# Attention and two MoE layers on one core: row sums in four streams, W_out blocks in the keys' place, and a new order

## Chip, cores and metric

One Trainium2 chip, one core. The metric is device microseconds of the core, the median of three runs. The profiled execution is one more run of the same kernel, and every row shown here is of that execution.

## What is computed

```python
def _attn_ref(q, k, v):                       # 2 batches, 12 heads, 448 tokens, head size 64
    scores = np.matmul(q, k.transpose(0, 1, 3, 2)) / np.sqrt(64)
    scores = np.where(np.triu(ones, k=1), -1e9, scores)
    attn = np.exp(scores - scores.max(-1, keepdims=True))
    return np.matmul(attn / (attn.sum(-1, keepdims=True) + 1e-09), v)

x = attn_out as 896 tokens x 768
h = x @ w_in                                  # 768 x 1024
solu = h * softmax(h)
x = layernorm(solu) * g_ln @ w_out            # 1024 x 768
out = relu(x @ w_in2)**2 @ w_out2             # 768 x 2048, 2048 x 768
```

The weights come as float64, read as pairs of 32-bit words.

## The kernel before

**Attention** goes over 12 pairs of heads, pair `i` holding two heads of 64 rows each (`h` is 0 or 1), so that K and Q of both fill 128 partitions. For each pair the kernel does the following, by the names in its order string. `S0a`, `S0b`, `S0c` (line 250) are cheap score products that only serve to find the row maxima, which VectorE (`mxa`, `mxb`, `mxc`, line 265), a transpose on TensorE (`mT`, line 277), ScalarE (`row`, line 282) and two small transfers (`rowd`, lines 294 and 295) turn into a row that a matmul subtracts. `Sa` and `Sb` (lines 308 and 319) are the full-precision scores, `ea1` and `eb1` (line 343) the exponentials on ScalarE, `ka` and `kb` (line 340) the causal mask on GpSimd. `ad` (lines 364 and 366) adds key blocks on GpSimd, so that the row sums need fewer columns on TensorE. `Ua` and `Ub` (line 352) multiply by V, with 64 output rows for each head, and `Us` (line 374) multiplies by ones, which gives the row sums in the second half of the same PSUM tile `U`.

**What follows a pair's sums** is a chain of small steps. `E` (lines 381 and 382) copies sums and products from PSUM to the SBUF tile `E`, of which there are two, and gives the PSUM tile back. `sums` (line 389) moves the sums of the two heads, each a row of 448 on one partition, into a 112x8 tile, one transfer for each head. `recips` (line 395) takes reciprocals on VectorE. `rcd` (line 401) writes them to DRAM, `spread` (line 408, two transfers) reads them back over 64 partitions for each head into the tile `bc`. `norm` (line 416) multiplies on GpSimd, and `x_hi` and `x_lo` (lines 424 and 428) split the result into two words.

**First MoE layer.** `h<t>.<c>` (line 492) adds the products of token tile `t` with the `c`-th of 6 blocks of `w_in`, six matmuls of 512 columns; it needs `x` of pair `c` (first batch), `6 + c` (second batch), or both for tile 3. A finished tile goes through `mx`, `ex`, `mu`, `sq`, `de`, `va`, `pw`, `fa`, `ln`, a transpose `T` (line 617) and a split `Th`, `Tl` (line 631). `lw` loads a block of `w_out` (768 KB, line 125), `of` (lines 150 to 152) makes float32 of it on VectorE, `oh` (line 564) and `ol` (line 567) split it. `y0` and `y1` (line 639) are its products. The second MoE layer (line 774) follows and is written as loops.

**Order.** Up to the second layer the string `SEQ` fixes the order, and with it the order on each engine and on the one queue (SP) from which all transfers are issued: an engine or queue takes its items in that order, and an item that waits holds up all behind it. `fl` items are matmuls on zeros at the start. PSUM holds four tiles in flight; a new one takes the place that was given back longest ago.

**Memory.** Blocks 0 to 5 of `w_out` have their place in the pool `lnp`, which is opened when the attention's last `x_lo` has been emitted, over tiles that the attention uses to its end.

Of the kernel before, what the change touches and what calls it, by code (L numbers as in the profile page):

```python
# [15 lines left out]
NEG = -3.0e38  # L16
UB_ = 3
NWO = 6
AHEAD = 2
NL2 = 3  # L20
LO_POOL = ()
# [3 lines left out]
ATT = ("recips", "rcd", "spread", "norm", "x_hi", "x_lo", "E", "Ua", "Ub", "sums")  # L25

SEQ = """
fl.0 fl.1 fl.2 load_r.0 fl.3 H.0 fl.4 load_r.1 fl.5 H.1 S0c.0 load_r.2 S0a.0 S0b.0 fl.6 fl.7 lq.0 load_r.3 lq.1 mxc.0
lq.4 mxb.0 S0b.1 load_v.0 S0a.1 fl.8 mxa.0 mxb.1 mxa.1 lq.2 mxr.0 Sa.0 H.2 ea1.0 S0c.1 mxc.1 S0a.2 S0b.2 mT.1 row.1
H.3 Sb.0 mxa.2 mxb.2 rowd.1 ka.0 eb1.0 S0c.2 mxc.2 S0b.3 Sb.1 load_r.4 mT.2 mxb.3 Ua.0 lq.5 eb1.1 kb.0 S0c.3 lq.3 ad.0  # L30
row.2 S0a.3 mxc.3 H.4 mxa.3 rowd.2 Sa.1 Ub.0 mT.3 ea1.1 Us.0 S0b.4 row.3 load_v.1 lq.6 wf.0 Sb.2 E.0 eb1.2 mxb.4 Sa.2
load_r.5 kb.1 ea1.2 rowd.3 S0a.4 ka.1 Sa.3 S0c.4 Sb.3 H.5 load_v.2 mxa.4 mxc.4 sums.0 S0a.5 ad.1 mT.4 load_r.6 lq.8
ea1.3 eb1.3 recips.0 mxa.5 row.4 Ua.1 S0b.5 ka.2 H.6 wh.0 Ub.1 S0c.5 lq.7 kb.2 mxb.5 rcd.0 S0a.6 mxc.5 load_v.3 rowd.4
Us.1 Sa.4 ad.2 load_r.7 kb.3 mxa.6 mT.5 E.1 row.5 S0b.6 ea1.4 Ua.2 Sb.4 H.7 mxb.6 S0c.6 spread.0 ka.3 sums.1 eb1.4
ad.3 mxc.6 S0a.7 Ub.2 mT.6 S0b.7 norm.0 kb.4 ld.3 row.6 ka.4 recips.1 mxa.7 x_hi.0 Us.2 rowd.5 E.2 Ua.3 Ub.3 x_lo.0
rcd.1 load_r.8 mxb.7 S0c.7 Sb.5 eb1.5 Sa.5 ad.4 H.8 mxc.7 rowd.6 mT.7 kb.5 Sb.6 ea1.5 wl.0 sums.2 row.7 Us.3 spread.1
recips.2 S0a.8 eb1.6 load_v.4 norm.1 Sa.6 rcd.2 load_r.9 rowd.7 x_hi.1 kb.6 Ua.4 ea1.6 Ub.4 E.3 ka.5 wf.1 S0b.8
spread.2 x_lo.1 Us.4 ka.6 mxa.8 load_r.10 sums.3 norm.2 H.9 S0c.8 ad.5 Sb.7 mxb.8 S0a.9 E.4 mxc.8 Sa.7 recips.3
load_v.5 eb1.7 mxa.9 S0b.9 x_hi.2 mT.8 Ua.5 ea1.7 S0c.9 ad.6 H.10 lq.9 rcd.3 mxb.9 Ub.5 load_v.6 sums.4 mxc.9 x_lo.2
S0b.10 row.8 Ua.6 mT.9 spread.3 load_r.11 Us.5 ka.7 norm.3 recips.4 row.9 mxb.10 rowd.8 wh.1 S0a.10 Ub.6 E.5 mxa.10  # L40
S0c.10 rcd.4 lq.10 kb.7 x_hi.3 load_g.0 H.11 mxc.10 x_lo.3 Us.6 wl.1 Sb.8 eb1.8 mT.10 Sa.8 ad.7 rowd.9 load_v.7 S0b.11
spread.4 sums.5 row.10 norm.4 lq.11 ea1.8 recips.5 mxb.11 E.6 Sa.9 Ua.7 load_v.8 rowd.10 S0a.11 Ub.7 kb.8 x_hi.4
S0c.11 ka.8 ea1.9 Us.7 rcd.5 mxa.11 Sb.9 mxc.11 mT.11 ld.4 row.11 spread.5 Sa.10 sums.6 eb1.9 x_lo.4 Ua.8 wf.2 rowd.11
ad.8 ka.9 Ub.8 h1.0 ea1.10 recips.6 rcd.6 wf.3 norm.5 Sb.10 E.7 ka.10 sums.7 x_hi.5 spread.6 eb1.10 load_v.9 kb.9
Sa.11 Us.8 x_lo.5 wh.2 wl.2 ld.5 Sb.11 h1.1 ea1.11 h1.2 h0.0 load_v.10 norm.6 E.8 recips.7 ad.9 Ua.9 eb1.11 Ub.9
x_hi.6 load_v.11 h0.2 Ua.10 Us.9 rcd.7 h0.1 sums.8 wf.4 kb.10 wh.3 wl.3 wh.4 h0.3 x_lo.6 spread.7 ka.11 wl.4 recips.8
norm.7 E.9 sums.9 wf.5 h0.4 ad.10 Ub.10 rcd.8 wh.5 x_hi.7 recips.9 h1.3 Ua.11 wl.5 x_lo.7 spread.8 h1.4 Us.10 h0.5
kb.11 mx.0 norm.8 rcd.9 E.10 ad.11 x_hi.8 ex.0 Ub.11 sums.10 spread.9 x_lo.8 recips.10 rcd.10 norm.9 de.0 h1.5 h2.0
h2.4 Us.11 mu.0 sq.0 h2.2 spread.10 h2.1 va.0 mx.1 E.11 x_hi.9 sums.11 pw.0 h2.3 fa.0 h2.5 x_lo.9 ln.0 T.0 ex.1
recips.11 norm.10 h3.0 h3.1 h3.3 x_hi.10 Th.0 rcd.11 de.1 spread.11 mx.2 mu.1 h3.2 ex.2 x_lo.10 sq.1 h4.0 Tl.0 norm.11  # L50
x_hi.11 h3.4 mu.2 x_lo.11 va.1 sq.2 de.2 h3.5 va.2 lw.0 pw.1 lw.1 fa.1 h4.1 pw.2 of.0 mx.3 fa.2 h4.4 ex.3 h4.2 ln.1
oh.0 of.1 mu.3 ln.2 ol.0 h4.3 sq.3 h5.0 oh.1 h5.4 de.3 T.1 lw.2 of.2 ol.1 oh.2 va.3 h4.5 pw.3 Th.1 mx.4 ex.4 T.2 h5.3
h5.2 fa.3 ln.3 h5.1 Tl.1 lw.3 Th.2 mu.4 h6.0 of.3 h5.5 lw.4 sq.4 h6.2 mx.5 h6.1 ex.5 oh.3 Tl.2 T.3 mu.5 Th.3 ol.2 h6.4
lw.5 Tl.3 of.4 de.4 de.5 sq.5 va.5 h6.3 pw.5 ol.3 h6.5 mx.6 va.4 fa.5 ex.6 lw.6 y0.0 of.5 pw.4 y0.1 oh.4 y0.2 l2.1
l2.0 oh.5 de.6 ol.4 mu.6 fa.4 of.6 y0.3 ln.4 ol.5 sq.6 oh.6 va.6 y0.4 ol.6 T.4 lw.7 pw.6 Th.4 Tl.4 y0.5 ln.5 fa.6 T.5
y0.6 ln.6 Th.5 of.7 Tl.5 oh.7 T.6 ol.7 Th.6 y0.7 Tl.6 f2.0 y1.0 f2.1 yo.1 y1.1 g2.1 yo.0 g2.0 yp.0 y1.2 yp.1 o2.1 yp.2
yo.2 o2.0 l2.2
"""


def attention_moe_kernel(tc, kq, v, w_in, w_out, g_ln, w_in2, w_out2, out):
# [16 lines left out]
    JP = 112  # L78
# [13 lines left out]
    with es:  # L92
# [21 lines left out]
        moe0, moe1 = ExitStack(), ExitStack()  # L114
# [55 lines left out]
        def give(t):  # L170
            slots.append(slot_of.pop(id(t))[0])
# [5 lines left out]
        with att:  # L177
# [4 lines left out]
            per = att_.enter_context(pool("per", side="right"))  # L182
            lat = att_.enter_context(pool("lat", side="right"))
# [13 lines left out]
            JK = [qk.tile([JP, JP * t + JP], mybir.dt.bfloat16, name=f"JK{t}") for t in range(4)]  # L197

            VR = [per.tile([P, 4, 2, D], F32, name=f"VR{i}") for i in range(3)]
            ONES = per.tile([P, D], F32, name="ONES")  # L200
            PP = [per.tile([P, 2, 512], F32, name=f"PP{i}") for i in range(NPP)]
            SE = per.tile([P, 1], F32, name="SE")
            Q2 = S - P
# [23 lines left out]
            nc.gpsimd.tensor_scalar_mul(NID, ident[0:JP, 0:JP], -1.0)  # L227
            nc.vector.memset(ONES, 1.0)

            mx = {}  # L230
            mr = {}
            UB = {}
            sb = {}
            ee = {}
            rr = {}
# [132 lines left out]
            def row_sum(i):  # L368

                p, pa = ps.pop(i), PP[(2 * i) % NPP]  # L370
                for o, x in ((0, pa[:, :, D : D + P]), (P, p)):
                    n = x.shape[2]
                    for h in range(2):
                        nc.tensor.matmul(
                            UB[i][D * h : D * h + D, 1, o : o + n], ONES, x[:, h], start=o == 0, stop=o > 0
                        )

            def u_out(i):
                U = UB.pop(i)
                ee[i] = lat.tile([P, 2, S], F32, tag="E", name="E", bufs=2)  # L380
                nc.scalar.activation(ee[i][0 : D + 1, 1], U[0 : D + 1, 1, 0:S], AF.Identity, bias=SE[0 : D + 1])
                nc.scalar.copy(ee[i][:, 0], U[:, 0, 0:S])  # L382
                give(U)

            def sums(i):
                c = lat.tile([JP, 8], F32, tag="sc", name="sc", bufs=2)
                for h in range(2):
                    r = ee[i][D * h : D * h + 1, 1].rearrange("o (p j) -> o p j", j=8)
                    nc.sync.dma_start(c[JP // 2 * h : JP // 2 * h + JP // 2], r)
                rr[i] = c  # L390

            def recips(i):
# [20 lines left out]
            def normalise(i):  # L413
                e, bc = ee.pop(i), rr.pop(i)
                x = lat.tile([P, S], F32, tag="x", name="x", bufs=1)
                nc.gpsimd.tensor_tensor(x, e[:, 0], bc, ALU.mult)  # L416
                xs[i] = x

            def x_parts(i):
# [133 lines left out]
            YB1 = {}  # L553

            def load_wo(fi):
                pl, tag, W, o = (M["lnp"], f"wo{fi}", 2 * DM, 0) if fi < NWO else (wst, f"w{fi - NWO}", 2 * DFF, 8)
                WO[fi] = load_w(pl, tag, w_out[fi * P : fi * P + P, :], W, o=o)

            def wo_f(fi):
# [235 lines left out]
            for n in range(NF2, N2):  # L795
                half, fi = blocks2[n]
# [4 lines left out]
                for e, d in sorted(order, key=lambda x: x[1]) if last else order:  # L801
# [3 lines left out]
                    c = ND * half + d  # L805
# [44 lines left out]
```

## Time and profile before

| | us |
|---|---|
| median of 3 runs | 452.52 (452.44 to 453.08) |
| profiled execution | 452.57 |
| its span in the trace | 450.7 |
| TensorE busy | 440.6 (98%) |
| VectorE, ScalarE, GpSimd busy | 265.2, 163.8, 151.5 |

The span is the time from the first to the last instruction that the trace shows; the execution's own time is 1.87 us longer. Busy time of TensorE counts a matmul to its modelled end, and matmuls overlap, so that a short wait can vanish behind the end of the matmul before.

### The profile page before, as it was taken

The numbers are of one execution on the slowest core, as the hardware profiler recorded it, in microseconds if no ns is written. First come the engines' busy times: TensorE is split into PE (matmuls) and PEld (weight loads), VectorE is DVE, ScalarE is ACT, GpSimd is POOL, SyncE is SP. The second block draws the span as 40 slices with busy tenths as digits, with TensorE's granted clock in tenths as the row PEclk, the third lists the DMA queues.
The fourth block names the chain that finished last, engine by engine and source line by source line (L and its number), as shares of the span: only waits on it lengthen the run. The fifth ranks groups of instructions, "written<-read, shape, count | busy, mean of one in ns | idle before, by whom it ended". The sixth has DMA issues, their size and how long they took to land.

```text
span 450.7 us, 6365 instructions
## 1 busy us (share of the span) xinstructions
PE 440.6 (98%) x2439; PEld 372.7 (83%) x2439; DVE 265.2 (59%) x511; ACT 163.8 (36%) x223; POOL 151.5 (34%) x145
## 2 busy tenths in 40 slices
PE   8999899999998999999999999999999999999996
PEld 6666455666886899888999999999999999999995
DVE  7887678955769996711456565675662424343221
ACT  3576655623638555311333342433331011210101
POOL 1599888894310011110113131322213132132310
PEclk9999999999999999999999999999999999999999
DMA  7476655501172180000033342424334243733403
GB/s 258 143 235 188 171 147 163 186 21 42 43 305 115 58 293 1 0 1 0 12 129 110 102 137 74 140 78 132 92 119 129 82 140 76 254 91 124 120 21 122
DMA packets 33288, 52.45 MB, mean 116 GB/s; under 512 B 6250, under 2 KB 24682, under 8 KB 32874
## 3 DMA queue, kind: packets, MB, share of 16 engines
q1 hardware_dynamic: 33258, 52.05, 36.6%
q8 instruction: 19, 0.31, 0.3%
q14 instruction: 11, 0.09, 0.1%
HBM read 49.16 MB, written 2.80 MB: 115 GB/s over the span
## 4 chain that ended last, share of the span: by engine, by line
PE 76%; POOL 8%; DMA 6%; DVE 5%; SPq 2%; ACT 1%; issue 1%; POOLq 0%; DVEq 0%
PE h L774 26%; PE o L774 26%; PE y L639 13%; PE h L492 5%; DMA bc<-d 3%; POOL PP L340 2%; POOL ps L364 2%; POOL ps L366 2%; POOL x L416 2%; PE s L308 2%; PE fill L521 1%; PE U L352 1%; DMA sc<-E 1%; DMA raw<-in_moe_w_out_dram 1%; SPq L408 1%
## 5 line engine op out<-in xcount | busy, mean ns | idle before, releaser
L695 POOL TENSOR_TENSOR w<-wf,w 128x768 fp32r<-128x768 f32 x32 | 59.2, 1848 | 204.4 <-ACT w L692 204.4
L774 PE MATMUL h<-yT,w 128*128 128x480 f32 x576 | 115.4, 362 | 0.0
L774 PE MATMUL o<-g,w 128*128 128x480 f32 x576 | 115.4, 362 | 0.0
L774 PEld LDWEIGHTS h<-yT,w 128*128 128x128 f32 x576 | 107.9, 187 | 7.4
L774 PEld LDWEIGHTS o<-g,w 128*128 128x128 f32 x576 | 107.9, 187 | 7.3
L150 DVE TENSOR_SCALAR wf<-raw 128x768 int32<-128x768 int32 (+1 forms) x46 | 28.5, 620 | 81.5 <-DMA raw<-in_moe_w_out_dram 57.3
L692 ACT CAST w<-wf 128x768 fp32r<-128x768 f32 x32 | 26.7, 836 | 134.4 <-DVE wf L152 121.9
L492 PE MATMUL h<-w,xT 128*128 128x512 f32 x252 | 61.3, 396 | 1.0 <-DVE lnT L631 1.0
L639 PE MATMUL y<-lnT,w 128*128 128x384 f32 (+1 forms) x288 | 58.5, 363 | 0.0
L492 PEld LDWEIGHTS h<-w,xT 128*128 128x128 f32 x252 | 46.2, 188 | 13.4 <-issue 4.0
L639 PEld LDWEIGHTS y<-lnT,w 128*128 128x128 f32 x288 | 51.9, 188 | 5.6
L152 DVE SCALAR_TENSOR_TENSOR wf<-raw,wf 128x768 int32<-128x768 int32 (+1 forms) x46 | 47.3, 1027 | 1.6
L151 DVE SCALAR_TENSOR_TENSOR wf<-raw,wf 128x768 int32<-128x768 int32 (+1 forms) x46 | 46.7, 1015 | 1.6
L265 DVE CUSTOM_DVE_ANT_0 JK<-mxp,MK 112x336 bf16<-112x336 f32 (+2 forms) x96 | 39.1, 445 | 10.8 <-PE mxp L250 9.9
L340 POOL TENSOR_SCALAR_AFFINE_SELECT PP<-PP 128x256 f32<-128x256 f32 (+1 forms) x48 | 28.5, 625 | 13.7 <-ACT PP L343 13.7
L308 PE MATMUL s<-KQ 64*128 64x448 f32 (+3 forms) x192 | 26.9, 398 | 1.4 <-ACT E L382 1.3
L343 ACT ACTIVATE PP<-s 128x1024 f32<-128x1024 f32 x24 | 24.4, 1023 | 9.9 <-PE s L319 7.5
L308 PEld LDWEIGHTS s<-KQ 64*128 64x128 f32 x192 | 16.6, 186 | 11.3 <-issue 5.4
L352 PE MATMUL U<-PP,VR 128*64 128x448 f32 (+3 forms) x192 | 25.1, 390 | 0.5 <-DMA VR<-in_v_dram 0.5
L756 DVE TENSOR_TENSOR relu<-h,relu 128x896 f32<-128x896 f32 x16 | 17.5, 1091 | 13.1 <-ACT relu L755 13.1
L366 POOL TENSOR_TENSOR ps<-ps,PP 128x384 f32<-128x384 f32 (+1 forms) x24 | 22.2, 926 | 1.9
L352 PEld LDWEIGHTS U<-PP,VR 128*64 128x64 f32 x192 | 11.5, 136 | 13.5 <-issue 7.6
(75 smaller groups left out, 359.7 us busy)
## 6 DMA issues: line engine op xcount, KB each, us to landing
raw<-in_moe_w_out_dram SPq DMA_DIRECT2D x24, 768.0 KB
raw<-in_moe_w_in_dram SPq DMA_DIRECT2D x16, 768.0 KB
KQ<-in_kq_dram SPq DMA_DIRECT2D x12, 448.0 KB
raw<-in_moe_w_in_dram SPq DMA_DIRECT2D x12, 256.0 KB
VR<-in_v_dram SPq DMA_DIRECT2D x12, 256.0 KB
raw<-in_moe_w_in_dram SPq DMA_DIRECT2D x3, 1024.0 KB
bc<-d SPq DMA_DIRECT2D x24, 112.0 KB
out_dram<-o SPq DMA_DIRECT2D x6, 240.0 KB
```

The source lines that it names most:

```text
L150: nc.vector.tensor_scalar(xi, hw, 3, 0x3FFFFFFF, ALU.logical_shift_left, ALU.bitwise_and)
L151: nc.vector.scalar_tensor_tensor(xi, hw, -0x40000000, xi, ALU.bitwise_and, ALU.bitwise_or)
L152: nc.vector.scalar_tensor_tensor(xi, lw, 29, xi, ALU.logical_shift_right, ALU.bitwise_or)
L265: nc.vector.tensor_tensor_reduce(JK[t], b[0:JP, h, o : o + nk], MK[:, S - nk :], 1.0, NEG, ALU.add, ALU.max, mx[i][:, 4 * h + t : 4 * h + ...
L308: nc.tensor.matmul(s[:, h, o : o + nq], K[r, P * t : P * t + P], Q[r, q0 : q0 + nq], start=t == HALF[a][0][0], stop=False,)
L340: nc.gpsimd.affine_select(ap, ap, [[0, 2], [1, m]], ALU.is_ge, 0.0, base=0, channel_multiplier=-1)
L352: nc.tensor.matmul(UB[i][D * h : D * h + D, 0, q0:S], VR[i % 3][:, t, h, :], PP[(2 * i + a) % NPP][:, h, o : o + nq], start=t == 0, stop=t ...
L366: nc.gpsimd.tensor_tensor(p[:, :, o:], p[:, :, o:], x, ALU.add)
L492: nc.tensor.matmul(b[:, half, :], xT[c][s][:, t * P : t * P + P], W1[c][:, w, 512 * half : 512 * half + 512], start=(c == 0 and s == 0 and ...
L639: nc.tensor.matmul(b[:, ci, 0:n], WO[fi][:, w, c * P : c * P + P], M["lnT"][a][s][:, fi, :], start=(fi == 0 and w == 0 and s == 0), stop=( ...
L695: nc.gpsimd.tensor_tensor(W2[n][:, 1], w_f["2", n], f(W2[n][:, 0]), ALU.subtract)
L774: nc.tensor.matmul(flat(b)[:, o : o + n], w[:, wp, c : c + P], ops[s][:, x : x + n], start=first and r == 0, stop=last and r == 2,)
```

## The change

**Row sums.** The 448 columns of each head are cut in two halves of 224. Each half of each head has 32 output rows of its own (ONES has 32 columns instead of 64): there are four streams of 224 columns in place of two of 448. The first half is two matmuls (128 and 96 columns), the second one matmul of 224. All of `U`'s sums then lie on partitions 0, 32, 64 and 96, `E`'s first instruction copies 97 x 224 in place of 65 x 448 elements into a tile of its own (`es`, two buffers), and `sums` is one transfer from four partitions in place of two. `spread` has two transfers before and after.

**W_out.** Blocks 0 to 3 get a pool `wo`, opened when the last pair's scores have been emitted, where the keys, queries and their parts were. Blocks 4 to 7 stay where they were.

**Order.** `SEQ` is new; the same 585 items stand in it. Counted from the two strings (a "block" is one TensorE item):

| | before | after |
|---|---|---|
| TensorE blocks | 176 | 176 |
| changes of the array's tile shape between blocks | 81 | 84 |
| blocks between `Us.i` and the block that takes the PSUM place which `E.i` gives back, i = 0 to 11 | 3 3 3 6 3 4 8 7 4 5 3 5 | 3 3 3 4 2 3 5 4 3 3 2 1 |
| `h` blocks (of 42) ahead of `Us.11` | 14 | 22 |
| blocks from `Us.11` to `h3.5`, the first that needs the last pair | 12 | 12 |
| `lw` issued before `spread.11` | none | `lw.0`, `lw.1`, `lw.2` |

`Us` stands directly behind a `Ub` in none of the pairs before and in four (1, 3, 9, 11) after.

```diff
+NWE = 4
...
+recips.7 h2.2 wf.5 kb.9 h2.3 wl.4 Sa.11 rcd.7 wh.5 sums.8 x_hi.6 spread.7 recips.8 h2.1 wl.5 h0.4 lw.0 x_lo.6 h0.5
+ea1.11 ad.9 Ua.9 Ub.9 rcd.8 mx.0 Us.9 norm.7 ka.11 h1.4 kb.10 of.0 E.9 h1.5 x_hi.7 mx.1 lw.1 ex.0 sums.9 ex.1 h2.4
+Ua.10 h2.5 ad.10 Ub.10 recips.9 mu.0 mu.1 sq.0 h5.0 sq.1 Us.10 x_lo.7 spread.8 h5.1 de.1 norm.8 rcd.9 h3.0 x_hi.8 lw.2
+kb.11 E.10 mx.2 x_lo.8 ex.2 Ua.11 ad.11 va.1 pw.1 h3.1 Ub.11 spread.9 de.0 norm.9 va.0 Us.11 sums.10 de.2 h5.2 oh.0
+recips.10 x_hi.9 E.11 mu.2 rcd.10 pw.0 ol.0 fa.1 h4.0 sq.2 h4.2 spread.10 of.1 x_lo.9 sums.11 recips.11 va.2 ln.1
+rcd.11 oh.1 fa.0 of.2 norm.10 spread.11 lw.3 h3.2 ln.0 h3.3 T.0 h5.3 x_hi.10 x_lo.10 h3.4 oh.2 pw.2 h4.3 ol.1 fa.2
...
-            ONES = per.tile([P, D], F32, name="ONES")
+            ONES = per.tile([P, D // 2], F32, name="ONES")
...
-                for o, x in ((0, pa[:, :, D : D + P]), (P, p)):
+                R, Q = D // 2, S // 2
+                for j, o, x in ((0, 0, pa[:, :, D : D + P]), (1, 0, p[:, :, Q - P :]), (0, P, p[:, :, 0 : Q - P])):
                     n = x.shape[2]
                     for h in range(2):
+                        r = D * h + R * j
                         nc.tensor.matmul(
-                            UB[i][D * h : D * h + D, 1, o : o + n], ONES, x[:, h], start=o == 0, stop=o > 0
+                            UB[i][r : r + R, 1, o : o + n], ONES, x[:, h], start=o == 0, stop=o + n == Q
                         )
...
-                nc.scalar.activation(ee[i][0 : D + 1, 1], U[0 : D + 1, 1, 0:S], AF.Identity, bias=SE[0 : D + 1])
-                nc.scalar.copy(ee[i][:, 0], U[:, 0, 0:S])
+                es_ = lat.tile([P, S // 2], F32, tag="es", name="es", bufs=2)
+                ee[i] = lat.tile([P, S], F32, tag="E", name="E", bufs=2)
+                n = P - D // 2 + 1
+                nc.scalar.activation(es_[0:n], U[0:n, 1, 0 : S // 2], AF.Identity, bias=SE[0:n])
+                nc.scalar.copy(ee[i], U[:, 0, 0:S])
...
-                for h in range(2):
-                    r = ee[i][D * h : D * h + 1, 1].rearrange("o (p j) -> o p j", j=8)
-                    nc.sync.dma_start(c[JP // 2 * h : JP // 2 * h + JP // 2], r)
+                r = rr.pop(i)[0 : P : D // 2].rearrange("k (p j) -> k p j", j=8)
+                nc.sync.dma_start(c, r)
...
+                M["wo"] = moe1.enter_context(pool("wo"))
...
-                pl, tag, W, o = (M["lnp"], f"wo{fi}", 2 * DM, 0) if fi < NWO else (wst, f"w{fi - NWO}", 2 * DFF, 8)
+                pl, tag, W, o = (M["wo" if fi < NWE else "lnp"], f"wo{fi}", 2 * DM, 0) if fi < NWO else (wst, f"w{fi - NWO}", 2 * DFF, 8)
```

## Rows read from the trace of the kernel before

**Rows 1.** The page: span, and busy time of each engine

```profile
span 450.7 us, 6365 instructions
...
PE 440.6 (98%) x2439; PEld 372.7 (83%) x2439; DVE 265.2 (59%) x511; ACT 163.8 (36%) x223; POOL 151.5 (34%) x145
```

**Rows 2.** Stretches: length, busy PE, PEld, DVE, ACT, POOL, granted clock, DMA share, GB/s

```profile
20.00:50.00 30.00, 30.00 (x263) 18.13 (x263) 24.23 (x83) 20.69 (x31) 29.21 (x40) 1.00 0.63 195
...
70.00:100.00 30.00, 30.00 (x195) 19.01 (x193) 24.98 (x29) 14.62 (x21) 26.59 (x23) 1.00 0.37 126
100.00:130.00 30.00, 30.00 (x149) 22.67 (x149) 16.63 (x39) 13.03 (x22) 10.60 (x13) 1.00 0.25 74
130.00:150.00 20.00, 18.28 (x87) 14.48 (x86) 19.45 (x33) 12.47 (x16) 0.55 (x1) 1.00 0.43 175
...
216.11:450.70 234.59, 230.44 (x1152) 215.50 (x1151) 114.09 (x132) 58.58 (x72) 55.46 (x30) 1.00 0.36 110
```

**Rows 3.** Waits of PE over the span: us in total, times, longest us

```profile
PE s L308 <- ACT E L382: 1.3, 1, 1.3
PE fill L521 <- DVE Z L212: 1.1, 1, 1.1
PE h L492 <- DVE lnT L631: 1.0, 1, 1.0
PE T L617 <- ACT h L588: 0.6, 1, 0.6
PE mxp L250 <- DVE mx L265: 0.6, 1, 0.6
PE U L352 <- DMA VR<-in_v_dram: 0.5, 1, 0.5
```

**Rows 4.** Timeline of PE around the row sums of pair 0

```profile
21.28 0.26 PE L277 MATMUL mxp<-ident,mx 112*8 112x112 f32 x1
21.47 0.44 PE L374 MATMUL U<-PP,ONES 128*64 128x128 f32 x4
21.74 0.71 PE L374 MATMUL U<-ps,ONES 128*64 128x320 f32 x4
22.38 0.48 PE L250 MATMUL mxp<-HI 64*128 64x336 f32 x4
```

**Rows 5.** Instructions of line 374: duration ns min/median/max, first and last start

```profile
L374 PE MATMUL U<-PP,ONES x48: 272/274/324, 21.5 to 110.6; 128*64 128x128 f32 x48
...
L374 PE MATMUL U<-ps,ONES x48: 432/432/433, 21.7 to 111.0; 128*64 128x320 f32 x48
```

**Rows 6.** The chain that ended last, 113 to 151 us: start, us, what

```profile
113.53 0.63 ACT E L381
...
115.50 1.95 DMA sc<-E
...
124.71 0.64 DVE xT L428
...
125.41 4.21 DMA raw<-in_moe_w_out_dram
...
129.65 0.57 DVE wf L150
...
132.19 1.13 DVE sm L575
...
145.13 5.73 PE h L492 x24
```

**Rows 7.** Waits of ACT over the span

```profile
ACT E L381 <- POOL x L416: 20.5, 7, 7.5
```

**Rows 8.** Timeline of the SP queue: the two transfers of pair 11's sums

```profile
114.65 1.65 SPq L389 DMA_DIRECT2D sc<-E  x2
```

**Rows 9.** Timeline of POOL: causal masks in two stretches

```profile
20.84 3.82 POOL L340 TENSOR_SCALAR_AFFINE_SELECT PP<-PP 128x256 f32<-128x256 f32 x4
...
27.75 1.37 POOL L340 TENSOR_SCALAR_AFFINE_SELECT PP<-PP 128x128 f32<-128x128 f32 x4
```

More of the change, by code (lines that the diff above doesn't have):

```diff
@@ L27 @@
 SEQ = """
[L28 to L57, printed above, removed]
+load_r.0 fl.0 fl.1 fl.2 H.0 fl.3 fl.4 S0c.0 fl.5 load_r.1 load_r.2 H.1 mxc.0 load_r.3 S0a.0 lq.0 fl.6 fl.7 S0b.0 S0a.1
@@ new lines @@
+fl.8 mxa.0 mxb.0 ld.3 S0b.1 mxr.0 H.2 mxa.1 mxb.1 Sa.0 load_v.0 S0c.1 H.3 S0b.2 S0b.3 mxc.1 ea1.0 mT.1 row.1 mxb.2
+Sb.0 S0a.2 ka.0 lq.4 S0c.2 mxb.3 rowd.1 lq.1 eb1.0 mxa.2 load_r.4 lq.2 Sa.1 S0a.3 ea1.1 Ua.0 mxc.2 mT.2 kb.0 Sb.1
+row.2 S0c.3 mxa.3 H.4 Ub.0 load_g.0 ad.0 eb1.1 mxc.3 ka.1 load_v.1 S0b.4 mT.3 rowd.2 Us.0 row.3 S0a.4 mxb.4 E.0
+load_r.5 Sa.2 kb.1 S0c.4 Sb.2 mxa.4 lq.3 ea1.2 sums.0 load_v.2 mxc.4 eb1.2 Ua.1 rowd.3 ad.1 mT.4 recips.0 Sb.3 Ub.1
+wf.0 Us.1 row.4 ka.2 H.5 lq.8 kb.2 eb1.3 rcd.0 S0a.5 Sa.3 E.1 load_r.6 ea1.3 ad.2 S0b.5 rowd.4 spread.0 ka.3 Sa.4
@@ new lines @@
+S0c.5 H.6 sums.1 mxa.5 mxb.5 lq.5 Sb.4 load_r.7 kb.3 S0a.6 recips.1 mxc.5 rcd.1 load_v.3 ea1.4 mT.5 norm.0 row.5 eb1.4
+Ua.2 S0b.6 Ub.2 lq.6 H.7 S0c.6 mxa.6 mxb.6 spread.1 ka.4 Us.2 x_hi.0 rowd.5 Ua.3 S0a.7 mxc.6 E.2 ad.3 mT.6 lq.7 sums.2
+x_lo.0 kb.4 load_r.8 S0b.7 load_v.4 wh.0 Ub.3 mxa.7 row.6 rowd.6 norm.1 Us.3 mxb.7 recips.2 S0c.7 Sb.5 E.3 x_hi.1 H.8
+Sa.5 mxc.7 sums.3 mT.7 row.7 eb1.5 Sa.6 rcd.2 wf.1 recips.3 ad.4 ea1.5 x_lo.1 S0b.8 kb.5 ea1.6 load_r.9 spread.2 Sb.6
+Ua.4 Ub.4 S0c.8 eb1.6 rowd.7 ka.5 mxb.8 H.9 norm.2 load_r.10 ad.5 S0a.8 mxa.8 rcd.3 Us.4 Sa.7 load_v.5 S0b.9 mxc.8 E.4
@@ new lines @@
+ea1.7 sums.4 Sb.7 mxb.9 S0a.9 mT.8 recips.4 kb.6 ka.7 Ua.5 spread.3 x_hi.2 row.8 S0c.9 Ub.5 H.10 load_r.11 rcd.4 mxa.9
+mxc.9 x_lo.2 S0a.10 mT.9 eb1.7 rowd.8 ka.6 norm.3 Us.5 S0b.10 ad.6 row.9 lq.9 wh.1 mxa.10 Sa.8 Sb.8 load_v.6 E.5 H.11
+mxb.10 rowd.9 load_v.7 S0c.10 wl.0 ea1.8 Ua.6 Ub.6 mxc.10 sums.5 kb.7 spread.4 S0b.11 x_hi.3 mT.10 recips.5 eb1.8
+lq.10 row.10 Us.6 rcd.5 load_v.8 S0a.11 x_lo.3 norm.4 mxb.11 lq.11 rowd.10 Sa.9 ad.7 Ua.7 load_v.9 spread.5 mxa.11
+wl.1 E.6 Ub.7 S0c.11 ka.8 Sb.9 ea1.9 mxc.11 x_hi.4 Sb.10 eb1.9 mT.11 Us.7 x_lo.4 h0.0 eb1.10 sums.6 wf.2 row.11 h1.0
@@ new lines @@
+norm.5 Sa.10 E.7 rowd.11 recips.6 wf.3 h1.1 ld.4 rcd.6 Ua.8 kb.8 ea1.10 Ub.8 ka.10 load_v.10 h0.1 wh.2 wl.2 h1.2 wh.3
+Sb.11 ad.8 wl.3 h0.2 x_hi.5 h0.3 ld.5 load_v.11 spread.6 sums.7 h1.3 Us.8 eb1.11 x_lo.5 wf.4 norm.6 wh.4 E.8 ka.9 h2.0
+recips.7 h2.2 wf.5 kb.9 h2.3 wl.4 Sa.11 rcd.7 wh.5 sums.8 x_hi.6 spread.7 recips.8 h2.1 wl.5 h0.4 lw.0 x_lo.6 h0.5
+ea1.11 ad.9 Ua.9 Ub.9 rcd.8 mx.0 Us.9 norm.7 ka.11 h1.4 kb.10 of.0 E.9 h1.5 x_hi.7 mx.1 lw.1 ex.0 sums.9 ex.1 h2.4
+Ua.10 h2.5 ad.10 Ub.10 recips.9 mu.0 mu.1 sq.0 h5.0 sq.1 Us.10 x_lo.7 spread.8 h5.1 de.1 norm.8 rcd.9 h3.0 x_hi.8 lw.2
@@ new lines @@
+kb.11 E.10 mx.2 x_lo.8 ex.2 Ua.11 ad.11 va.1 pw.1 h3.1 Ub.11 spread.9 de.0 norm.9 va.0 Us.11 sums.10 de.2 h5.2 oh.0
+recips.10 x_hi.9 E.11 mu.2 rcd.10 pw.0 ol.0 fa.1 h4.0 sq.2 h4.2 spread.10 of.1 x_lo.9 sums.11 recips.11 va.2 ln.1
+rcd.11 oh.1 fa.0 of.2 norm.10 spread.11 lw.3 h3.2 ln.0 h3.3 T.0 h5.3 x_hi.10 x_lo.10 h3.4 oh.2 pw.2 h4.3 ol.1 fa.2
+h4.4 Th.0 Tl.0 T.1 ol.2 norm.11 x_hi.11 ln.2 x_lo.11 h3.5 Th.1 of.3 mx.3 h4.1 oh.3 h4.5 h5.4 Tl.1 T.2 ex.3 mu.3 de.3
+h5.5 lw.4 sq.3 mx.4 h6.0 Th.2 va.3 pw.3 ex.4 mx.5 fa.3 h6.3 Tl.2 ln.3 mu.4 h6.1 T.3 ex.5 mu.5 de.4 Th.3 h6.4 sq.5 Tl.3
@@ L58 @@
+h6.2 sq.4 of.4 ol.3 lw.5 h6.5 oh.4 va.4 pw.4 mx.6 of.5 y0.0 ol.4 ex.6 de.5 mu.6 va.5 fa.4 oh.5 sq.6 de.6 y0.1 ln.4
+lw.6 y0.2 va.6 pw.6 y0.3 l2.1 ol.5 pw.5 T.4 of.6 fa.5 oh.6 y0.4 Th.4 lw.7 fa.6 ln.5 y0.5 ln.6 ol.6 Tl.4 of.7 T.5 Th.5
+oh.7 Tl.5 l2.0 l2.2 ol.7 y0.6 T.6 Th.6 Tl.6 f2.0 y0.7 y1.0 yo.0 y1.1 g2.0 yp.0 yo.2 o2.0 yo.1 f2.1 yp.1 g2.1 o2.1 y1.2
+yp.2
 """
@@ L379, in u_out @@
                 U = UB.pop(i)
-                ee[i] = lat.tile([P, 2, S], F32, tag="E", name="E", bufs=2)
-                nc.scalar.activation(ee[i][0 : D + 1, 1], U[0 : D + 1, 1, 0:S], AF.Identity, bias=SE[0 : D + 1])
-                nc.scalar.copy(ee[i][:, 0], U[:, 0, 0:S])
+                es_ = lat.tile([P, S // 2], F32, tag="es", name="es", bufs=2)
[3 more added lines that the diff above has]
+                nc.scalar.copy(ee[i], U[:, 0, 0:S])
+                rr[i] = es_
                 give(U)
@@ L415, in normalise @@
                 x = lat.tile([P, S], F32, tag="x", name="x", bufs=1)
-                nc.gpsimd.tensor_tensor(x, e[:, 0], bc, ALU.mult)
+                nc.gpsimd.tensor_tensor(x, e, bc, ALU.mult)
                 xs[i] = x
```

## The prediction

> **What bounds the kernel now.** I read the page first. TensorE is busy 440.6 of 450.7 us, and no other engine comes near [rows 1]. The table of stretches shows where that holds. The second layer, from 216.11 us on, keeps PE at 230.44 of 234.59 us, and what is missing there is the last copy and store after the last matmul; none of its code is changed, so those 234.6 us stand. Before it, PE is full in the stretches 20 to 50, 70 to 100 and 100 to 130 us, all at the full granted clock of 1.00, and has a hole of 1.7 us in 130 to 150 [rows 2]. In the first half GpSimd is nearly as full (29.21 of 30 us) while TensorE is full too, so GpSimd is the runner-up there, and VectorE (19.45 of 20) is it in 130 to 150 [rows 2]. The view of PE's waits then names the holes. The six groups come to 5.1 us, of which 1.1 is the start [rows 3]. So the kernel is TensorE's own work plus about 4 us of holes, and an edit gains only if it takes work from TensorE or closes a hole.
>
> **Row sums on TensorE.** The trace shows what a pair's block costs: it starts at 21.47 and the next block at 22.38, 0.91 us [rows 4]. A record of 128 columns takes 272 ns and one of 320 takes 432 [rows 5], so a column costs (432 - 272) / 192 = 0.833 ns. There are 96 records [rows 5] for 48 matmuls, so each matmul is run in two passes. Two heads side by side need (128 + 320) x 2 x 0.833 = 747 ns if they overlap in full, and that fits in the 0.91 us only if they do. What is left, 0.16 us, is the cost of changing the array's shape on the way in and out (0.27 - 0.21 on the first four records and 0.64 - 0.53 on the last four [rows 4]).
>
> Afterwards each of four streams has 224 x 2 x 0.833 = 373 ns. No row shows four streams of 32 columns. If all four overlap, a block gains 747 - 373 = 373 ns, 4.5 us over 12 pairs. If only two overlap at a time, the passes add up to the same 747 ns and nothing is gained; I see no row by which it would lose more than the few ns between neighbouring records. In between lies the case that passes start only in the order of issue. Streams three and four would then begin when the first pair's second pass does, 128 x 0.833 = 107 ns late, and the gain is 267 ns, 3.2 us in all. Since the two streams of today run side by side without loss, I take a value between the upper two: **-3.8 us** (0 to -4.5).
>
> The Trainium skill bears on that choice: its page "TensorE: Matmul & The Clock Gate", Part 3, "The mechanism", says that matmuls keep their program order at start and at end. By that rule the gain would be the 3.2 us of the ordered case, and the total 0.6 us higher than mine; no row here shows four streams, so it is open.
>
> **Shape changes.** The new order has 84 of them for 81. Three more at the 0.16 us just read are **+0.5 us**.
>
> **The copy and the transfers of the sums.** E's first instruction took 0.63 us for 448 columns [rows 6]; with half the columns it cannot be longer, and at best it halves. Two issues on SP took 1.65 us, 0.82 each [rows 8]; one replaces them, which could cost from 0.82 to 1.65 since it moves the same 112 pieces. Landing took 1.95 us [rows 6]; from four partitions it may take longer, at most twice that by the same row. I price all of these at nothing for the end: they lie in the chain from E to x_lo, which runs beside TensorE's work. In pair 11 that chain took from 113.53 to 125.35 us, 11.8 us [rows 6], and TensorE stayed full over 100 to 130 us [rows 2]. In the new order nine h blocks of 5.73 / 4 = 1.43 us [rows 6] and two transposes stand between Us.11 and h3.5, the first that needs pair 11: at least 12.9 us of cover, 1.1 more than the chain. If the cover went, the 0.8 us saved (or the 1.95 us lost) per pair would count once, at the last pair.
>
> **W_out in the keys' place.** Today lw.0 can only go out once x_lo.11 is done: the chain shows x_lo at 124.71, the transfer from 125.41 for 4.21 us, conversion from 129.65 to 132.19 (2.5 us a block), and then VectorE's mixture of conversions and layer norm until TensorE, waiting, takes h at 145.13 [rows 6]. That mixture is the hole of 1.0 us behind lnT, and the 0.6 us at T behind the square is in the same stretch [rows 2, 3]. In the new order of.0, of.1 and of.2 come before Tl.0, so 3 x 2.5 = 7.5 us of conversion leave that stretch for 100 to 130, where VectorE has 13.4 of 30 us free [rows 2]. I count both holes as closed: **-1.6 us**. Bounds: 0, if VectorE only runs into the same wait elsewhere, and -1.6. What pays for it are three issues of lw between the small transfers of pairs 8 to 10. A block of 768 KB lands after 4.21 us with five more behind it [rows 6]; a small transfer queued behind one block is at most that much later. rcd.8, sums.9 and spread.9 stand directly behind one each. Behind rcd.8 and sums.9 wait recips, spread and norm of those pairs, then x_hi (ScalarE) and E.10, E.11.
>
> **The new order.** In attention three holes come from late small things: 1.3 us behind E's copy, 0.5 behind a load of V, 0.6 behind the maxima [rows 3], 2.4 us in all. E's copy is late because ScalarE waits for norm of two pairs before, which has to leave the tile E; that happened 7 times for 20.5 us, and one of them reached TensorE [rows 3, 7]. The order moves loads earlier and shortens SP's work. But the number of blocks that cover E has not grown: 3 to 8 before, 1 to 5 after. I take half of the 2.4 us as closed, **-1.2 us** (0 to -2.4), and leave **+1.0** for one new wait of the 1.3 us kind where the cover is thin (Ua.11 and h4.0 stand two blocks and one behind the Us whose E they need). The start keeps its fills and its first load; I count nothing.
>
> **Sum.** -3.8 + 0.5 - 1.6 - 1.2 + 1.0 = -5.1 us against the profiled execution's 452.57, which is 450.7 of span and 1.87 around it; the median is 452.52, so there is no correction. Forecast: **447.5 us**. All gains in full and no new wait would be -4.5 + 0.5 - 1.6 - 2.4 = -8.0, 444.6. None of the gains, with the shape changes and the new wait, is +1.5, 454.1.
>
> **Rivals.**
>
> 1. Four streams don't run together. The change then does what it says in code and not on the array: 447.5 + 3.8 = 451.3. For it: the trace has no such case. Against it: two streams overlap within the 0.16 us of rest.
>
> 2. GpSimd sets the pace. If TensorE needs 0.3 us less for each pair, GpSimd with 29.21 of 30 and 26.59 of 30 us [rows 2] is next in attention. It is also not steady: four masks took 3.82 us at one place and 1.37 at another [rows 9], so what runs beside them decides. For it: norm.0 and norm.1 now stand ahead of ad.3 and ad.4 in GpSimd's order, where they stood behind, and a late bc would hold ad up. Against it: from 100 us to 130 us it has 19 of 30 us free [rows 2]. Price: half to all of the 3.8 us, 449.4 to 451.3.
>
> 3. Slower, through E and the PSUM places. ScalarE waits for norm in E; a PSUM place comes back late; TensorE stops. Today one of seven such waits gets through, for 1.3 us [rows 3, 7]. With covers of 1 to 5 blocks all seven could: 447.5 - 1.0 + 7 x 1.3 = 455.6. It decides from the sixth on (446.5 + 6 x 1.3 = 454.3 is slower, five give 453.0). For it: the shorter covers and the W_out blocks ahead of small transfers. Against it: pair 11's chain of 11.8 us fits between Us.8 and Us.10, where eleven h blocks alone take 15.7 us.
>
> **Chances.** What this kernel's timing can tell from no change is about 0.2%, 0.9 us: 451.6 to 453.4. The forecast gets 0.58, with its own range 444.6 to 449.4. Rival 1 gets 0.10, half of it within 0.2%. Rival 2 gets 0.14, nearly all faster. Rival 3 gets 0.16: 0.13 slower, the rest same. The last 0.02 lie under the forecast's range. Faster 0.58 + 0.05 + 0.13 + 0.02 = 0.78, same 0.09, slower 0.13. The range runs from 444.4, all gains in full, through rivals 1 and 2 into the first part of rival 3, 453.2; it leaves out some 0.16, nearly all above.
>
> **What would show it.** Row sums: a pair's block should take 0.91 - 0.32, about 0.6 us, to the next block's start, and the records of 224 columns of both heads should start with those of 128; if they start 0.2 us or more later, rival 1 holds. W_out: the wait of h for lnT gone and of.0 before 125 us. Order: PE's waits before 216 us at 2 to 3 us instead of 4, and the first matmul of the second layer near 211 us. GpSimd: in rival 2 it would be at 9.5 tenths or more all through 20 to 90 us with TensorE waiting for masks. Rival 3 would show as PE waiting for ACT E more than once. I would be wrong above all if the new order holds a wait that I can't see from the old trace, since the order's part of the sum rests on counts and not on a timed run.

## The result and the profile after

The changed kernel takes **446.19 us** in the median (445.59 to 449.13, 4 runs) against 452.59 for the kernel before: ratio 0.9874, 95% interval 0.9834 to 0.9913. Its profiled execution took 445.59 us, 443.9 of them span. Single runs of it lie further apart than those of the kernel before (0.6 us), here and in the repeats below (up to 455.17), and why is open.

The page gives span and busy time, and the line on TensorE answers to [rows 1].

```profile
span 443.9 us, 6457 instructions
...
PE 435.9 (98%) x2487; PEld 372.0 (84%) x2487; DVE 268.6 (61%) x511; ACT 162.8 (37%) x223; POOL 151.9 (34%) x145
```

6.8 us of span went, 4.7 of them as busy time of TensorE. The view of PE's waits of the changed kernel, over its whole span, answers to [rows 3]:

```profile
PE fill L526 <- DVE Z L213: 1.1, 1, 1.1
PE mxp L251 <- ACT HI L241: 1.0, 2, 0.5
PE U L353 <- DMA VR<-in_v_dram: 0.7, 1, 0.7
PE s L309 <- ACT PP L344: 0.4, 1, 0.4
PE mxp L278 <- DVE mx L266: 0.4, 1, 0.4
```

The waits behind E's copy, the layer norm and the square, and that of a score product (`mxp`, line 250) for the maxima, which were there in [rows 3], are gone (the 0.4 us that a transpose waits for the maxima were there before, too); 2.5 us of waits are left besides the start, and 1.7 of them are loads that come late: HI waits 0.5 us for the first keys and 0.5 us, at 21.8 us, for pair 4's, and U waits for V. The timeline of PE around pair 0's row sums answers to [rows 4]:

```profile
22.22 0.26 PE L278 MATMUL mxp<-ident,mx 112*8 112x112 f32 x1
22.41 0.30 PE L377 MATMUL U<-PP,ONES 128*32 128x128 f32 x2
22.42 0.38 PE L377 MATMUL U<-ps,ONES 128*32 128x224 f32 x2
22.54 0.28 PE L377 MATMUL U<-PP,ONES 128*32 128x128 f32 x2
22.64 0.36 PE L377 MATMUL U<-ps,ONES 128*32 128x224 f32 x6
22.92 0.47 PE L251 MATMUL mxp<-HI 64*128 64x448 f32 x2
```

The two streams of 224 columns start 0.01 us behind the two of 128 (a row counts the two heads, and each matmul has two passes), so all four run side by side. From the block's start to the next block's it is 0.51 us, where it was 0.91. Summed over the 12 blocks in the same way, 10.74 us became 6.19.

The stretches up to the second layer's first matmul, of the kernel before and of the changed one (length, then busy PE, PEld, DVE, ACT, POOL, clock, DMA share, GB/s), in one fence each:

```profile
0.00:215.95 215.95, 210.01 (x1288) 157.08 (x1288) 151.15 (x379) 105.22 (x151) 95.99 (x115) 1.00 0.38 124
```

```profile
0.00:209.14 209.14, 205.28 (x1335) 156.38 (x1336) 155.91 (x381) 104.90 (x153) 96.43 (x115) 1.00 0.40 128
```

The whole 6.8 us lie here: 4.7 less busy, and idle time of TensorE down from 5.9 to 3.9. The second layer takes 234.7 us, as before.

### The profile page after: what moved, and what is told of

The parts are those of the page before. It is cut to its first block, busy times and chain, and to the rows that moved or that the text cites. A ratio compares the mean times of both kernels' runs of the same rounds, so it can differ in the third digit from the quotient of the medians.

```text
span 443.9 us, 6457 instructions
## 1 busy us (share of the span) xinstructions
PE 435.9 (98%) x2487; PEld 372.0 (84%) x2487; DVE 268.6 (61%) x511; ACT 162.8 (37%) x223; POOL 151.9 (34%) x145
## 4 chain that ended last, share of the span: by engine, by line
PE 92%; DMA 3%; POOL 2%; ACT 1%; SPq 0%; issue 0%; DVE 0%; POOLq 0%; ACTq 0%
PE h L780 26%; PE o L780 26%; PE h L497 14%; PE y L645 13%; PE s L309 4%; PE U L353 4%; DMA KQ<-in_kq_dram 2%; PE mxp L251 1%; PE T L623 1%; PE U L377 1%; DMA VR<-in_v_dram 1%; PE s L320 1%; PE s L328 1%; POOL x L421 1%; PE fill L526 0%; ACT HI L241 0%
## 5 line engine op out<-in xcount | busy, mean ns | idle before, releaser
L152 DVE SCALAR_TENSOR_TENSOR wf<-raw,wf 128x768 int32<-128x768 int32 (+1 forms) x46 | 49.0, 1064 | 1.6
L153 DVE SCALAR_TENSOR_TENSOR wf<-raw,wf 128x768 int32<-128x768 int32 (+1 forms) x46 | 46.1, 1002 | 1.6
L341 POOL TENSOR_SCALAR_AFFINE_SELECT PP<-PP 128x256 f32<-128x256 f32 (+1 forms) x48 | 26.4, 579 | 17.8 <-ACT PP L344 17.8
L367 POOL TENSOR_TENSOR ps<-ps,PP 128x384 f32<-128x384 f32 (+1 forms) x24 | 24.7, 1030 | 1.9
```

Source lines behind the costliest of these rows:

```text
L152: nc.vector.scalar_tensor_tensor(xi, hw, -0x40000000, xi, ALU.bitwise_and, ALU.bitwise_or)
L153: nc.vector.scalar_tensor_tensor(xi, lw, 29, xi, ALU.logical_shift_right, ALU.bitwise_or)
L341: nc.gpsimd.affine_select(ap, ap, [[0, 2], [1, m]], ALU.is_ge, 0.0, base=0, channel_multiplier=-1)
```

## Experiments

Medians of the kernel before beside these runs were 453.04, 452.90 and 453.01 us in three groups of four kernels; each group ran on one chip.

**again** and **again2: the changed kernel unaltered.**

> The changed kernel once more, unaltered, because its four runs lay 3.5 us apart (445.59 to 449.13) and those of the kernel before only 0.6. If the spread belongs to the new order (TensorE waits for loads that land at another time in each run), it shows again: a median of 446 to 447, single runs up to 449, and another set of waits for loads in the trace than 1.0 us for HI and 0.7 us for VR. If it was an accident of one chip, all runs lie within 0.7 us of 445.6.

> The changed kernel unaltered, on the chip of these runs, to compare with and to see its spread once more. By the runs so far a median of 446 to 447, with about one run in three 3 us or more above the fastest; if the trace is of such a run, TensorE's matmuls should take twice their time in some stretch of the first 20 us, as in the one slow trace.

446.48 us (445.35 to 455.17; ratio 0.9863, interval 0.9827 to 0.9900) and 446.00 (445.12 to 447.55; 0.9844, 0.9822 to 0.9867). The trace of again2 is of the run of 447.55, with 445.8 us of span, 1.9 more than the changed kernel's first trace. Much of that is loads that land later. In its view of PE's waits they are

```profile
PE U L353 <- DMA VR<-in_v_dram: 1.4, 1, 1.4
PE mxp L251 <- ACT HI L241: 1.4, 3, 0.7
```

where the first trace has 0.7 and 1.0: 1.1 of the 1.9 us.

**rows_only: the row sums alone.** `SEQ` and the place of W_out as before; ONES, the matmuls, `es`, `E` and the one transfer as changed.

> Only the row sums of the change (four streams, one transfer of the sums, smaller tiles), with the order and the place of W_out of before. Theory: TensorE's time is the time, so the 12 blocks that fell from 10.74 to 6.19 us in sum give 4.5 us, less 0.2 for two more changes of tile shape: 448.3. Rival (GpSimd or the chain of small transfers sets the pace, and the gain comes from the order): at least half of the 4.5 us is lost in new waits of TensorE, 450.5 or more.

446.89 us (446.60 to 447.43), ratio 0.9867, interval 0.9847 to 0.9886. That is 6.1 us, nearly all of the change, and more than TensorE's blocks give. Its trace has no wait of TensorE between 120 and 160 us, although W_out still waits there for the last x_lo.

**two_streams: order and place without the row sums.**

> The changed kernel with the row sums of before (two streams of 64 columns, two transfers of the sums, the larger tiles), the order and the place of W_out new. Theory: 446.2 + 4.5 = 450.7, so that order and place alone are worth some 1.9 us. Rival (gain comes from the order): 448.5 or less. If order and place need the faster sums to close the holes, it is slower than 451.5.

453.82 us, ratio 1.0018, interval 0.9995 to 1.0041: no gain at all, if anything 0.8 us lost. Both theory (450.7) and rival (448.5) are wrong. With the old sums the new order has more waits in attention than the old one: 1.9 us behind HI, 1.0 for V and 0.8 for the row MR, and the 1.2 us behind E's copy are still there.

**rows_two and one_transfer: the two halves of the row sums.** The first keeps four streams and sends the sums in two transfers, the second keeps two streams and sends them in one; order and place as before in both.

```diff
# one_transfer
-                for h in range(2):
-                    r = ee[i][D * h : D * h + 1, 1].rearrange("o (p j) -> o p j", j=8)
-                    nc.sync.dma_start(c[JP // 2 * h : JP // 2 * h + JP // 2], r)
+                r = ee[i][0 : D + 1 : D, 1].rearrange("k (p j) -> k p j", j=8)
+                nc.sync.dma_start(c, r)
# rows_two, against rows_only
-                r = rr.pop(i)[0 : P : D // 2].rearrange("k (p j) -> k p j", j=8)
-                nc.sync.dma_start(c, r)
+                e_ = rr.pop(i)
+                for h in range(2):
+                    r = e_[D * h : D * h + D : D // 2].rearrange("k (p j) -> k p j", j=8)
+                    nc.sync.dma_start(c[JP // 2 * h : JP // 2 * h + JP // 2], r)
```

> Four streams in the old order and with W_out in the old place, but the sums of the two heads in two transfers as before: TensorE's saving without the transfer's. Theory (each is worth something by itself, and they overlap in the holes they close): between the kernel before less TensorE's 4.5 us, 448.4, and 1.5 us more if the shorter blocks of TensorE turn into waits for the sums: 448 to 450. Rival (the transfer adds nothing once the streams are four): 446.9, as the row sums alone.

> The kernel before with one edit: the sums of the two heads go out in one transfer from two partitions in place of two transfers. TensorE's work is unchanged. The row sums alone, in the old order and with W_out in the old place, had no hole left between 125 and 150 us. Theory (those holes close because the chain from E to x_lo got shorter): 452.9 - 1 = about 451.5, and the two holes shrink. Rival (they close because TensorE's own blocks are shorter): 452.5 to 453.2, both holes still there. If the single transfer lands later than two, slower.

rows_two: 448.47 us, ratio 0.9905 (0.9883 to 0.9926), 4.5 us. one_transfer: **449.38 us**, ratio 0.9917 (0.9895 to 0.9939), 3.5 us without any work taken from TensorE. I had expected 1 us. In one_transfer TensorE has no wait between 120 and 160 us. These are left:

```profile
PE s L308 <- ACT E L382: 1.2, 1, 1.2
PE fill L520 <- DVE Z L212: 1.1, 1, 1.1
PE mxp L277 <- DVE mx L265: 0.5, 1, 0.5
PE mxp L250 <- ACT HI L240: 0.4, 1, 0.4
```

The first step behind the transfer is the reciprocal on VectorE. Its waits for the sums up to 150 us, in the kernel before, one_transfer, rows_two and the changed kernel:

```profile
DVE sr L395 <- DMA sc<-E: 10.2, 5, 4.6
```

```profile
DVE sr L394 <- DMA sc<-E: 2.8, 4, 1.5
```

```profile
DVE sr L401 <- DMA sc<-es: 2.8, 2, 1.9
```

```profile
DVE sr L400 <- DMA sc<-es: 1.7, 3, 0.7
```

This wait is a sign of the trouble and not its size: rows_two, with two transfers, waits as little as one_transfer does, and rows_only waits 2.6 us and is still 1.6 us faster than rows_two. Where one_transfer gains shows when its TensorE records are laid beside those of the kernel before, 2439 in each. Its span is 3.3 us shorter, and it gets ahead in three ways.

At 56 us it gains 0.7 us, by a load of V. In the queue of the kernel before this load stands behind `rcd` (line 401), and `rcd` waits for the reciprocal:

```profile
54.10 0.34 SPq L401 DMA_DIRECT2D d<-sr  x1
54.49 0.42 SPq L209 DMA_DIRECT2D VR<-in_v_dram  x1
```

In one_transfer the same load goes out at 53.74 us.

At 70 us it gains 0.7 us, by the maxima. VectorE takes its items in order, and here they stand behind a reciprocal that waits for the sums, with TensorE waiting for the maxima in turn. The chain of the kernel before:

```profile
66.14 1.96 DMA sc<-E
...
68.22 0.20 DVE sr L395
68.42 0.38 DVE JK L265
...
69.78 0.47 PE mxp L250 x2
```

From 136 to 145 us it gains 2.1 us: the holes at T and at h, 0.6 and 1.0 in [rows 3], and a few tenths ahead of them. The chain from E to the last x_lo ends 3.3 us sooner, at a time when TensorE is 1.2 us ahead, and the loads of W_out, which need the place that the attention gives back with it, go out at 122.12 us in place of 125.41 [rows 6]:

```profile
122.12 2.07 SPq L125 DMA_DIRECT2D raw<-in_moe_w_out_dram  x4
```

That the early W_out closes these two holes is also what place_only shows, below.

On the SP queue a pair's sums cost 1.65 us in two issues [rows 8]; the one issue takes 0.57 in one_transfer and 0.60 in the changed kernel, here its line in the view of that source line (ns min/median/max):

```profile
L394 SPq DMA_DIRECT2D sc<-es x12: 586/602/628, 23.5 to 118.0; - x12
```

**sums_two: the changed kernel with two transfers.** The edit is that of rows_two, on the changed kernel.

> The changed kernel with the sums of the two heads in two transfers again, all else as changed. Theory (the reciprocals stand in VectorE's order ahead of maxima and layer norms, and wait for the sums): VectorE's waits for sc rise from 1.7 us towards the 10.2 us of the kernel before, and the time to 447.5 to 449.5. Rival (the new order has slack enough for the second transfer): 446.3, as the changed kernel.

447.91 us (446.07 to 454.46), ratio 0.9878 (0.9852 to 0.9904); by the ratios that is some 1.5 us more than the changed kernel beside it (0.9844). The direction is the theory's, but the intervals of the two ratios overlap, so the size is loose. The way is not shown to be the theory's: VectorE's wait for the sums rose to 3.4 us only, and what TensorE has here and not in the changed kernel's first trace are waits for E's copy and for GpSimd, besides 0.3 us for the row MR:

```profile
PE s L309 <- ACT E L387: 0.7, 1, 0.7
PE U L353 <- POOL ps L365: 0.5, 1, 0.5
```

**place_only, rows_place and wout_late: the place of W_out.** place_only adds the pool to the kernel before, rows_place to rows_only, and wout_late takes it away from the changed kernel (`NWE = 0`, lw.0 to lw.3 directly behind the last x_lo, and of, oh, ol of blocks 0 to 3 spread by my hand between the layer norms).

> The kernel before with blocks 0 to 3 of W_out in the keys' place and nothing else, the order unchanged: lw.0 still stands behind spread.11, but needs no longer wait for the last x_lo. Theory (as predicted for the place): the conversions start some 4 us earlier, both holes of 0.6 and 1.0 us at 138 and 144 us close, about 451.2. Rival: VectorE meets the next layer norm at the same time anyway, or the three loads delay pair 11's last transfers: 452.5 to 453.2.

> Row sums and the place of W_out as changed, the order as before. What is left to the changed kernel is the order alone. Theory: with the sums faster no hole was left between 125 and 150 us, so the place gives nothing here: 446.9, and the order some 0.5 us. Rival (the place is what the changed kernel gained over the row sums alone): 446.3 or less.

> The changed kernel with blocks 0 to 3 of W_out in their old place, so that their loads go out after the last pair's x_lo and their conversions stand among the layer norms as before; all else new. Theory: the waits of h behind lnT and of T behind the square come back, some 1.6 us: 447.8, with TensorE waiting 1 to 2 us between 125 and 150 us. Rival (the new order has slack enough there, and the place is worth nothing): 446.2, TensorE without a wait in that stretch.

place_only: 451.57 us, ratio 0.9963 (0.9944 to 0.9983), so 1.3 us, and its trace has no wait of TensorE between 120 and 160 us. That trace is of a run of 452.82 us, though, with the same span of 450.7 us as the kernel before: what the two holes gave went into attention, where the waits for E's copy (1.3 us before) and for the maxima (0.6) had grown.

```profile
PE s L309 <- ACT E L383: 2.2, 2, 1.2
PE mxp L251 <- DVE mx L266: 1.6, 1, 1.6
```

rows_place: 446.82, ratio 0.9869 (0.9848 to 0.9890), the same as rows_only. The place closes the two holes, and so does the single transfer; whoever comes second finds them closed.

wout_late: 456.84 us, ratio 1.0116 (1.0072 to 1.0159), 10 us more than the changed kernel where I expected 1.6. The stretches of its trace, in the columns of [rows 2]:

```profile
120.00:140.00 20.00, 20.00 (x113) 15.99 (x110) 6.49 (x18) 9.04 (x12) 4.37 (x5) 1.00 0.31 108
140.00:165.00 25.00, 16.21 (x68) 12.78 (x67) 24.25 (x39) 13.81 (x19) 0.55 (x1) 0.80 0.52 191
```

VectorE is idle for two thirds of 120 to 140 us and full to 24.25 of 25 us after it, and TensorE waits, at one transpose for 8.1 us:

```profile
PE T L622 <- ACT u L616: 8.1, 1, 8.1
```

Beside the changed kernel's trace TensorE falls 8.4 us back in this hole, and another 2.3 by 163.6 us, with the clock at its lower level. More h blocks than before stand ahead of Us.11 in the new order, so less is left behind it under which four conversions could hide; that is argued from counts. With the conversions where I put them, the new order needs the early W_out. How much of the 10 us is my placing was not tried apart.

**fills_six and best: the spread, and three loads.** fills_six is `fl.5` ahead of `S0c.0`; best is that and `lq.1` behind `load_r.4`, `lq.2` behind `load_v.1`, `load_v.6` ahead of `load_r.11`.

> The changed kernel with one edit: the sixth pair of fill matmuls stands before the first score product again, as in the kernel before, and not behind it. In the slow one of the traces of the new order TensorE's matmuls took twice their time from 5.5 to 20.4 us, and the new order has a hole of 0.3 to 0.5 us at 5 us, where the sixth fill used to be. Theory (the hole lets some runs keep the lower clock): runs between 445 and 447, none above 448, and no hole at 5 us. Rival (the runs of 449 to 455 come from loads that land late): as before, about one run in three lies at 449 or more.

> As the kernel with the sixth fill first, and three loads moved in the queue: two parts of W_in behind the load of pair 4's keys and the load of V after it, and the load of V for pair 6 ahead of that of pair 11's keys. TensorE waited 0.5 us for the first and 0.7 us for the last. Theory: both waits go, 1.0 us under the kernel with the sixth fill first, about 444.7. Rival: a transfer lands when the 16 engines have room, and the waits only move to another load: no difference.

fills_six: 445.72 us (445.41 to 448.67), ratio 0.9858 (0.9827 to 0.9890). The hole at 5 us is gone, and 448.33 and 448.67 us are still among the six times, so my theory of the spread fell; nor did any reach the 449 of the rival. The granted clock of these two was 0.992 and 0.995 in the mean, that of the other four 0.998 to 1.000. best: **445.10 us** (444.15 to 448.82), ratio 0.9832 (0.9800 to 0.9863), the lowest of all. In its trace, of a span of 442.4 us, TensorE does not wait for V, and the 0.4 us that it waits for HI are at 5.4 and 7.6 us and no longer for pair 4's keys at 21.8:

```profile
PE s L309 <- ACT PP L344: 0.4, 1, 0.4
PE mxp L251 <- ACT HI L241: 0.4, 2, 0.2
```

The two waits did go, as the theory has it. But the medians of fills_six and best differ by only 0.6 us, and their intervals overlap with each other and with those of the changed kernel (ratios 0.9844 to 0.9874), so that best beats either is likely and not shown.

## Why the prediction was right

The total was forecast at 447.5 with a range of 444.4 to 453.2, and it is 446.2. (All gains in full come to 444.6 by the sum, and not to the 444.4 of the range; nothing hangs on it.) The sum was right in its first term and wrong in where the rest came from; that the total came so near is in part luck, because the gain of the transfer, which is missing from it, and the 1.6 us for W_out's place, of which the other edits leave nothing, make up for each other.

**Row sums on TensorE** (-3.8): the mechanism was right and the size somewhat small. All four streams overlap, which is the upper bound of 4.5; the 12 blocks shrank by 10.74 - 6.19 = 4.55 us. rows_two gained as much, 4.5, but has more than this term: E's first copy took 0.45 us in place of 0.63, and each of its two issues for the sums 0.56 in place of 0.81; and its trace has new waits in attention beside smaller holes at W_out. Rival 1 is out. The ordered case is out as well: the Trainium skill ("TensorE: Matmul & The Clock Gate", Part 3, "The mechanism") says that matmuls keep program order at start and end, and by my reading streams three and four would have begun 107 ns late; in the trace they begin 10 ns after the first two, ahead of those streams' second passes at 22.54. What fell is my reading, that a matmul's second pass goes ahead of the next matmul's first: the first passes of the four do begin in the order of the program, so the rule for starts is not contradicted (the ends in these rows are modelled). The claim of the same section of the Trainium skill, that tiles of the array run side by side, is what these rows show.

**The transfer of the sums** (priced at nothing): this is the step that failed. "They lie in the chain from E to x_lo, which runs beside TensorE's work" looks only at whether the chain is covered at the last pair. On its way the chain holds up other things: a load of V behind `rcd` in the queue, maxima behind the reciprocal on VectorE, and the loads of W_out that wait for the last x_lo. The trace of before had a sign of it in a view that I did not bring into the sum: 10.2 us of VectorE waiting for sc. Alone the single transfer is worth 3.5 us; on top of four streams 448.47 - 446.89 = 1.6. The issue was mispriced as well: 0.57 to 0.60 us is less than the 0.82 that I took for its least.

**W_out in the keys' place** (-1.6): the holes are real and the place closes them, for 1.3 us alone. But the single transfer closes them too, and on top of the row sums, in the old order, the term is zero (446.82 against 446.89).

**The order** (-1.2 + 1.0) and the shape changes (+0.5): the order as changed, on top of the other two, gives 446.82 - 446.00 = 0.8 us on the same chip, with intervals that overlap; the shape changes are in that, and no run measures them alone. Their price was too high by its own working: the 0.16 us were read from a block's way in and out, which is two changes, and were charged for each of three. My claim that the order by itself closes half of the waits in attention is wrong: with the old sums it has more of them (two_streams), and by the ratios two_streams is some 2.5 us slower than place_only (1.0018 against 0.9963, intervals apart, each beside the kernel before on its own chip), from which it differs by the order alone.

Taken one after the other, the terms are 4.5 (four streams, with the shorter E), 1.6 (one transfer), 0.1 (place) and 0.8 (order), 7.0 in sum, which is 453.01 - 446.00; taken in another order they would differ, and rows_only ran on another chip than the rest. I reached 5.1 by terms of which one was missing, one counted what another closes, and one was a guess.

**Rivals 2 and 3.** GpSimd did not set the pace: rows_two gained 4.5 us, with 0.8 us of TensorE waiting for ps, and in the changed kernel TensorE waits for GpSimd nowhere. ScalarE's wait for norm ahead of E, 20.5 us in [rows 7], has no line in the changed kernel's waits at all, so thin covers did no harm there. In two_streams E's copy held TensorE once, for 1.2 us, which is the size I gave such a wait.

**Open.** E's shorter copy and the four streams were not tried apart. And the traced execution of wout_late (462.89 us) lies 6 us above its median because of its start, in the timeline of PE:

```profile
7.67 1.86 PE L525 MATMUL fill<-Z 128*128 128x448 f32 x4
```

The same four fills take this in the changed kernel's first trace, and the first ten there, in the next line, 0.39 us each:

```profile
6.75 1.03 PE L526 MATMUL fill<-Z 128*128 128x448 f32 x4
1.10 3.90 PE L526 MATMUL fill<-Z 128*128 128x448 f32 x10 [1.10 <-DVE Z L213]
```

Behind the first of a group, a fill takes 581 ns in the first 4 us of both traces, and 353 to 356 in the changed kernel from 6 us on. So wout_late goes on at the pace of the first fills, up to 20.4 us, and that costs 6.2 us by then. The clock column shows 1.00 for this stretch, but it shows 1.00 for 1 to 3 us of the changed kernel as well:

```profile
1.00:3.00 2.00, 1.90 (x5) 1.75 (x6) 1.60 (x8) 1.06 (x1) 1.44 (x5) 1.00 0.29 78
```

The first record of the clock in the trace begins at 4.65 us there and at 20.41 us in wout_late, in both where the matmuls become faster, and ahead of it the column says nothing. By the fills' times TensorE ran at the lower of its two levels until then. Why the clock rose so late in that run is not settled.

## What to carry to other kernels

A small step that sits off the bound engine's path is not free if it shares an in-order engine or queue with work that the bound engine waits for, or if a later load needs the place that the step's chain gives back: look up who waits for the step's transfer in the waits of every engine, not only in those of the bound one. Price edits that close the same hole once, and find out by doing each alone. An order is fitted to the durations it was made for: this one is worth some 0.8 us with the new sums and costs some 2.5 with the old.

## What was not expected of the hardware

One transfer from two or four partitions in place of two transfers issued in 0.57 to 0.60 us, less than either of the two did alone (0.82 each [rows 8]), for the same 112 pieces. The number of pieces is not what sets it: rows_two has two transfers of 56 pieces again, each from two partitions, and they issue faster than those of the kernel before, from one partition each. First before, then rows_two:

```profile
L389 SPq DMA_DIRECT2D sc<-E x24: 762/807/861, 23.5 to 115.5; - x24
```

```profile
L395 SPq DMA_DIRECT2D sc<-es x24: 505/557/592, 24.2 to 111.4; - x24
```

With one source partition an issue took 0.81 us, with two 0.55 to 0.57, with four 0.60; why is not shown.

Four streams of 32 columns lose nothing against each other: the block's 0.51 us is 0.14 above the 373 ns that one stream's columns need, and the block of two streams was 0.16 above its 747.

In wout_late the granted clock of 140 to 165 us was 0.80 in the mean, a mixture of the levels 2.4 and 1.2 GHz, around the hole of 8.1 us; in 120 to 140 us, without a hole, it was 1.00. Behind the hole a transpose took 428 ns in the mean, against 272 in the changed kernel.
